# Streamed weights in DRAM: from slice by slice to partition by partition, 81 KB apart

## The chip, the cores and the metric

The kernel runs on one core of one Trainium2 chip. The metric is device time in microseconds (us) of one execution; the lower, the better. "PE" is TensorE, "DVE" VectorE, "ACT" ScalarE, "POOL" GpSimd and "SP" SyncE, whose queue issues the loads that this study is about.

## The reference, cut to what matters

Two branches read the same 2048 tokens of width 640 and are mixed by a gate. Branch A is attention with a sliding window. Branch B is recurrent: 64 segments of 32 tokens, each preceded by 8 memory tokens that the segment before has produced.

```python
for s in range(n_seg):                      # 64 segments, one after the other
    h = concatenate([mem, xs])              # 8 + 32 tokens
    q, k, v = h @ Wq, h @ Wk, h @ Wv        # each 640 x (32 heads * 192)
    ...                                     # softmax(q k^T) v
    o = o @ Wo                              # (32 * 192) x 640
    mem = o[:, :M]                          # needed by the next segment
```

The four matrices together take more room than the on-chip memory (SBUF) has left. Most slices of them stay resident; 21 slices are read from DRAM again in each segment.

## The kernel before

The streamed slices are packed once into a DRAM tensor `w_packed`. A slice is 128 partitions by 1536 bf16 values (q, k, v: 3072 B for a partition) or 1280 (o: 2560 B).

```python
KINDS = ("q", "k", "v", "o")
WQ, WO = 4 * 384, 2 * D

class Weights:
    def __init__(self, nc, dram, Wq, Wk, Wv, Wo, streamed):
        ...
        self.slot = {u: n for n, u in enumerate(streamed)}       # 21 slices
        self.packed = dram.tile([len(streamed), P, WQ], BF, name="w_packed")
    ...
    def dram_of(self, u):
        return self.packed[self.slot[u], :, 0:self.width(u)]
```

So a slice was one block of 384 KB, with the 128 rows one behind the other. The recurrent branch reads it into a ring of four buffers:

```python
sb = {"w": (4, [P, WQ]), ...}                                    # ring of 4
def load_w(u):
    if u not in weights.slot:
        return None                                              # resident
    b = sc.buf("w")
    sc.op("SP", 100 + 0.78 * weights.width(u),
          lambda: nc.sync.dma_start(tile_of(b)[:, 0:weights.width(u)], weights.dram_of(u)), writes=[b])
    return b
```

A fixed list schedule orders all instructions when the program is built; its costs are not measured on the chip, so the layout in DRAM does not alter the order.

## Time and profile before

| Quantity, kernel before | Value |
|---|---|
| time, median of 4 runs | 2614.36 us (2612.79 to 2619.13) |
| span of the profiled run | 2624.0 us |
| recurrent stage, from its first segment (the stream's first load is issued at 699.0 us) to 4 us after the issue of the last load | 708.6 to about 2588 us |
| one segment | 29.37 us |
| loads of the stream | 1344 (21 for each of 64 segments) |
| TensorE busy / DMA engines busy in the stage | 86% / 86% |
| chain of waits, loads of the stream | 32% of the span |

How to read it: the stage from 700 to 2590 us is most of the span, and in it both TensorE and the DMA engines are nearly full.

### The profile page before, as it was taken

What the parts mean: (1) busy time and instruction counts of PE and PEld (TensorE: products, weight loads), DVE (VectorE), ACT (ScalarE), POOL (GpSimd) and SP (SyncE); (2) the same over time, 40 slices, a digit from 0 to 9 for tenths busy, and PEclk for the clock granted to TensorE, in tenths of its full rate; (3) what the DMA queues carried; (4) which work ended last, traced back from release to release, by engine and by line L of the source; (5) the groups of instructions that cost most, each with busy time, mean ns of one, the idle gap of its engine ahead of it and who ended that gap; (6) DMA issues with size and microseconds to landing.
All of it is one profiled execution on the core that took longest, in us unless ns stands there. A gap on an engine that the chain in (4) does not pass through costs nothing.

```text
span 2624.0 us, 113795 instructions
## 1 busy us (share of the span) xinstructions
PE 2259.0 (86%) x49877; PEld 1665.6 (63%) x49893; DVE 1189.0 (45%) x3578; ACT 1115.8 (43%) x2433; POOL 602.1 (23%) x1782
## 2 busy tenths in 40 slices
PE   7888888899788888888888888888888888888885
PEld 5777777699465666666655665666666665566663
DVE  5777777623243344434443343434443444334433
ACT  5777777722233333333333333333333333334333
POOL 7622222040122222222222222222222222122220
PEclk9999999999899999989999998999999999999997
DMA  6600000085588888888888888888888888888887
GB/s 215 196 17 17 20 17 15 21 262 150 158 277 264 284 276 264 288 275 281 266 276 271 284 268 266 274 282 275 270 285 272 275 282 273 264 269 283 279 274 236
DMA packets 299154, 591.76 MB, mean 226 GB/s; under 512 B 102552, under 2 KB 112032, under 8 KB 298656
## 3 DMA queue, kind: packets, MB, share of 16 engines
q1 hardware_dynamic: 275536, 525.43, 63.6%
q0 software_dynamic: 20160, 55.60, 6.5%
q8 instruction: 391, 6.41, 1.0%
q10 hardware_dynamic: 2960, 3.44, 0.4%
q14 instruction: 107, 0.88, 0.1%
HBM read 554.98 MB, written 36.97 MB: 226 GB/s over the span
## 4 chain that ended last, share of the span: by engine, by line
PE 51%; DMA 35%; ACT 10%; DVE 2%; issue 2%; SPq 0%; ACTq 0%; POOL 0%; DVEq 0%
DMA t_w<-w_packed 32%; PE ps_q L597 8%; PE ps_k L597 8%; PE ps_o L762 7%; PE ps_v L597 5%; ACT a_ex L195 4%; PE t_psum L438 4%; ACT a_pt L208 3%; PE qk_ps L124 3%; PE ps_pv L738 2%; PE tr_k L612 2%; PE t_psv L455 2%; PE S_ps L666 2%; PE pt_ps L205 1%; PE s_ps L187 1%
## 5 line engine op out<-in xcount | busy, mean ns | idle before, releaser
L597 PEld LDWEIGHTS <-t_hT 128*32 128x32 bf16 x15360 | 380.0, 99 | 310.2 <-issue 105.8
L762 PE MATMUL ps_o<-t_OT,t_w 128*128 128x40 bf16 x6400 | 270.6, 182 | 124.9 <-DMA t_w<-w_packed 113.7
L762 PE MATMUL ps_o<-t_OT,w_o 128*128 128x40 bf16 x8960 | 334.6, 182 | 42.0 <-ACT t_OT L743 41.7
L762 PEld LDWEIGHTS <-w_o 128*128 128x128 bf16 x8960 | 289.1, 98 | 49.5 <-issue 43.5
L762 PEld LDWEIGHTS <-t_w 128*128 128x128 bf16 x6400 | 210.6, 98 | 155.4 <-DMA t_w<-w_packed 152.1
L743 ACT CAST t_OT<-ps_pv 128x480 bf16<-128x480 f32 x256 | 143.2, 559 | 340.2 <-PE ps_pv L738 339.9
L195 ACT ACTIVATE a_ex<-s_ps,a_nmx 128x384 bf16<-128x384 f32 (+2 forms) x512 | 252.8, 576 | 64.2 <-DVE a_nmx L193 61.5
L644 POOL COPY t_K<-t_xqk 128x64 bf16<-128x64 bf16 x256 | 60.8, 237 | 947.8 <-PE S_ps L666 665.6
L193 DVE TENSOR_REDUCE a_nmx<-s_ps 128x1 f32<-128x384 f32 (+2 forms) x512 | 246.7, 523 | 32.4 <-PE s_ps L190 24.8
L602 ACT CAST t_tok<-ps_k 128x384 bf16<-128x384 f32 x256 | 122.7, 479 | 319.5 <-PE ps_k L597 319.5
L597 PE MATMUL ps_q<-w_q,t_hT 128*32 128x384 bf16 x4096 | 230.4, 348 | 18.7 <-DVE t_hT L773 18.4
L721 DVE TENSOR_TENSOR t_PTx<-PT_ps,mk_x 128x320 bf16<-128x320 f32 x256 | 125.2, 489 | 264.7 <-PE PT_ps L714 264.7
L597 PE MATMUL ps_v<-w_v,t_hT 128*32 128x384 bf16 x4352 | 230.1, 335 | 0.0
L597 PE MATMUL ps_k<-w_k,t_hT 128*32 128x384 bf16 x4096 | 226.3, 343 | 0.3
L635 DVE COPY t_K<-tr_k 128x256 bf16<-128x256 bf16 x256 | 74.0, 289 | 253.7 <-PE tr_k L612 252.4
L602 ACT CAST t_tok<-ps_q 128x384 bf16<-128x384 f32 x256 | 123.0, 481 | 137.7 <-PE ps_q L597 137.5
L187 PE MATMUL s_ps<-KT_blk,QTm 128*128 128x128 bf16 x1440 | 171.0, 223 | 6.0 <-ACT a_ex L195 5.6
L602 ACT CAST t_vtok<-ps_v 128x384 bf16<-128x384 f32 x256 | 122.7, 479 | 114.2 <-PE ps_v L597 112.9
L612 PEld LDWEIGHTS <-t_tok 128*128 128x128 bf16 x1536 | 87.7, 98 | 118.7 <-ACT t_tok L602 55.4
L773 DVE CAST t_hT<-ps_o 128x40 bf16<-128x40 f32 x63 | 12.6, 200 | 327.1 <-PE ps_o L762 327.1
L205 PE MATMUL pt_ps<-a_ident,a_ex 128*128 128x128 bf16 x1440 | 145.6, 220 | 8.5 <-ACT a_ex L195 1.2
L676 DVE TENSOR_REDUCE sm_mx<-S_ps 128x4 f32<-128x160 f32 x256 | 82.5, 322 | 149.0 <-PE S_ps L666 149.0
(138 smaller groups left out, 4606.2 us busy)
## 6 DMA issues: line engine op xcount, KB each, us to landing
t_w<-w_packed SPq DMA_DIRECT2D x704, 384.0 KB, 4.4
t_w<-w_packed SPq DMA_DIRECT2D x640, 320.0 KB, 4.3
xbqk<-t_qk SPq DMA_DIRECT2D x16, 768.0 KB, 5.1
t_xqk<-xbqk POOLq DMA_DIRECT2D x64, 192.0 KB, 4.7
w_v<-in_B_Wv_dram POOLq DMA_DIRECT2D x17, 384.0 KB, 7.1
w_q<-in_B_Wq_dram POOLq DMA_DIRECT2D x16, 384.0 KB, 5.2
w_k<-in_B_Wk_dram POOLq DMA_DIRECT2D x16, 384.0 KB, 6.5
xbv<-t_vt SPq DMA_DIRECT2D x64, 96.0 KB, 1.8
```

The lines of the kernel that those rows point to most:

```text
L187: nc.tensor.matmul(sp[:, ci * P:(ci + 1) * P], lhsT=qm[r][:, g, :], rhs=kring[c][:, g, :], start=True, stop=not need_mask)
L193: nc.vector.tensor_reduce(out=nmx[:], in_=sp[:, 0:nk * P], axis=AX.X, op=ALU.max, negate=True)
L195: nc.scalar.activation(out=ex[:, 0:nk * P], in_=sp[:, 0:nk * P], func=ACT.Exp, bias=nmx[:], scale=1.0)
L205: nc.tensor.transpose(pt_ps[:, a, ci, :], ex[:, ci * P:(ci + 1) * P], ident[:])
L438: nc.tensor.matmul(pt[:, bb, :], lhsT=ws[ki][kt][:, c:c + P], rhs=xTb[:, kt, t * P:(t + 1) * P], start=(kt == 0), stop=(kt == KT - 1))
L597: nc.tensor.matmul(t[32 * j:32 * j + 32, 0:384], lhsT=tile_of(hT)[:, kt, :], rhs=w[:, j * 384:(j + 1) * 384], start=(kt == kts[0]), stop=( ...
L602: sc.op("ACT", act(384), lambda: nc.scalar.copy(tile_of(tok)[:], b["tile"][:, 0:384]), reads=[b], writes=[tok])
L612: nc.tensor.transpose(t[:, k, :], tok["tile"][:, k * P:(k + 1) * P], ident[:])
L676: nc.vector.tensor_reduce(out=x["mx"][:], in_=view(), axis=AX.X, op=ALU.max)
L721: nc.vector.tensor_tensor(out=tile_of(dst)[:], in0=PT["tile"][:, i, :, :].unsqueeze(2).to_broadcast([P, 2, 4, L]), in1=mk.unsqueeze(1).uns ...
L743: sc.op("ACT", act(480), lambda: nc.scalar.copy(tile_of(OT)[:].rearrange("p b j l -> p (b j l)"), o["tile"][:, 0:480]), reads=[o], writes= ...
L762: nc.tensor.matmul(t[:, dt * L:(dt + 1) * L], lhsT=w[:, r * D + dt * P:r * D + (dt + 1) * P], rhs=OT["tile"][:, b, i, :], start=(g == 0 an ...
```

## The change

The intent is to lay the streamed weights out by partition: in DRAM, all slices of partition 0 lie side by side, then those of partition 1, and so on. The tensor has 27 slots where 21 are used, so that neighbouring partitions are 27 x 3072 = 82944 B (81 KB) apart.

```diff
-        self.packed = dram.tile([len(streamed), P, WQ], BF, name="w_packed")
+
+        assert len(streamed) <= 27
+        self.packed = dram.tile([P, 27, WQ], BF, name="w_packed")
@@
     def dram_of(self, u):
-        return self.packed[self.slot[u], :, 0:self.width(u)]
+        return self.packed[:, self.slot[u], 0:self.width(u)]
```

## The prediction

> **What bounds the kernel now.** I read the page's slices first, then the stage table, the chain of waits, the DMA issues, and last the durations of single DMA packets.
>
> The slices show three phases: the sliding-window branch (to about 525 us, with next to no DMA from 128 us), the tail projections (525 to 700 us), and the recurrent branch (700 to 2590 us), which is 72% of the span.
>
> ```profile
> PE   7888888899788888888888888888888888888885
> ...
> DMA  6600000085588888888888888888888888888887
> GB/s 215 196 17 17 20 17 15 21 262 150 158 277 264 284 276 264 288 275 281 266 276 271 284 268 266 274 282 275 270 285 272 275 282 273 264 269 283 279 274 236
> ```
>
> Only the third phase streams weights all the time. The stage table (us, busy of PE, PEld, DVE, ACT, POOL, then clock, DMA share, GB/s) has for it:
>
> ```profile
> 700.00:2590.00 1890.00, 1634.09 (x40453) 1140.43 (x40453) 750.80 (x2627) 690.83 (x1603) 399.04 (x1369) 0.94 0.86 274
> ```
>
> Two things are nearly full at once: TensorE (1634 of 1890 us, 86%) and the 16 DMA engines (86%). Which of them ends the steps is told by the chain and by the waits:
>
> ```profile
> DMA t_w<-w_packed 32%; PE ps_q L597 8%; PE ps_k L597 8%; PE ps_o L762 7%; PE ps_v L597 5%; ACT a_ex L195 4%; PE t_psum L438 4%; ACT a_pt L208 3%; PE qk_ps L124 3%; PE ps_pv L738 2%; PE tr_k L612 2%; PE t_psv L455 2%; PE S_ps L666 2%; PE pt_ps L205 1%; PE s_ps L187 1%
> ...
> PEld L762 <- DMA t_w<-w_packed: 152.1, 269, 2.2
> ...
> PE ps_o L762 <- DMA t_w<-w_packed: 113.7, 178, 2.1
> ```
>
> The weight stream is the largest single item, 32% of the span or 840 us. TensorE idles for it too (113.7 us at the output projection, and some 39 us at the q, k and v matmuls). So the stage is bound by a loop of both: the stream goes through a ring of 4 buffers, and a load is issued when TensorE has finished with the buffer it overwrites. The queue that issues the loads shows it, waiting for TensorE and for landings in turn:
>
> ```profile
> SPq L565 <- PE ps_o L762: 327.6, 528, 2.4
> ...
> SPq L565 <- DMA t_w<-w_packed: 307.9, 446, 2.8
> ```
>
> The stream itself:
>
> ```profile
> t_w<-w_packed SPq DMA_DIRECT2D x704, 384.0 KB, 4.4
> t_w<-w_packed SPq DMA_DIRECT2D x640, 320.0 KB, 4.3
> ```
>
> That is 1344 loads, 21 for each of 64 segments. The copies of the new memory into t_hT start at 738.1 and at 2558.8 us, 62 segments apart, so a segment takes 29.37 us and a load comes every 1.40 us. With 4.35 us from issue to landing, 4.35/1.40 = 3.1 of the 4 buffers are in flight at any time.
>
> The records of single packets say how good these transfers are. The stage has 90107 packets of 3072 B and 81920 of 2560 B, one per partition row. Their medians, 121 and 102 ns, are practically their minimum: 3072/121 = 25.4 B/ns for one engine, 406 GB/s for 16. The means are 154.7 and 125.7 ns, because about one packet in ten stalls, mostly for 100 to 800 ns. In time of all 16 engines: (90107 x 154.7 + 81920 x 125.7)/16 = 1515 us of packets in the stage, of which 1204 us would be left with every packet at its median. **The stalls are 311 us, and only they can answer to where the rows lie in DRAM.** I sorted packets into 16 engines by fitting starts to ends (an inference, the record has no engine number). Packets that follow another without a gap hold 206 us of the stalls. Most of the rest follow a gap, where the delay of a first read is exposed; I don't expect the layout to change that.
>
> **What the Trainium skill says.** "Perfetto Trace Analysis", section "Contiguity and DMAs", says that contiguity matters only within an SBUF partition line. By that, 128 rows of 3072 B cost the same adjacent or 81 KB apart. The trace agrees only in part: rows are separate packets even now, though their DRAM bytes are adjacent, so no merging can be lost; nothing in it shows distant rows at this rate. "DMA: Bandwidth & Descriptors", section "Latency and other measured facts", reports that the row pitch does matter where it is a large power of two (207 GB/s at 512 KiB, 103 at 4 MiB, and full rate again with 4 KiB more). 81 KB = 82944 B is 81 x 1024, far smaller and an odd multiple, so that penalty should not be met. No trace here shows such a pitch. "HBM Reference", section "Specifications", gives about 716 GB/s for the memory that two cores share. This core alone draws 274 GB/s, so raw memory bandwidth is not short, which the 406 GB/s of the median packet supports.
>
> **The change part by part.**
> 1. Instructions. I compared the built programs engine by engine: the sequences are identical but for line numbers. The 1344 loads, their widths, the ring of 4, the queue and all waits stay. Removed: nothing; added: nothing. Issue stays about 320 ns a load on a queue that mostly waits. 0 us.
> 2. Packets. Each partition's row is still 3072 or 2560 B contiguous, so their number and the 1204 us at median stay. 0 us.
> 3. Filling the packed copy: 51 transfers of 80 or 384 KB at 77 to 123 us, DRAM to DRAM, with a scattered destination now. The stream's first read comes at 519 us, so even doubled times (2.7 to 9.1 us each) are hidden. 0 us.
> 4. First reads in the tail projections: 11 loads of 3.5 us. A change of 10% in each would be 4 us at most.
> 5. Stalls in the recurrent stage, the only real term. Before, one load reads a solid block of 384 KB, and the next in flight comes from another block. After, it reads 128 rows spread over 10.4 MB. In favour: streams of the 16 engines spread differently over memory, and the diff pads 21 slices to 27, so somebody chose the pitch with care; 21 slices would have given 63 KB, almost 64.[...] I choose a small gain, a quarter of the 206 us: 52 us of DMA time.
>
> How much of that reaches the end? The chain contains 840/4.35 = 193 landings, about 3 of the 21 in a segment. If a load needs x less DMA time, its landing, behind 3.1 in flight, comes about 3.1x earlier, and the chain gets 193 x 3.1x = 598x shorter, while DMA time falls by 1344x. **So about 0.45 of what the engines save reaches the end**; a slowdown could pass through fully, as DMA then becomes the sole bound. 52 x 0.45 = 23 us. With some weight for exactly nothing: 2614 - 16 = 2598 us.
>
> **Rivals.**
> - *Nothing happens.* The stalls come from refresh or from competing traffic, not from addresses. For it: they strike packets alike at all places, and the contiguous reads of t_xqk stall little less (146.8 ns mean against 154.7 for the same size). Time 2605 to 2620.
> - *Row conflicts vanish.* If half of the 206 us go, 103 x 0.45 = 46 us, 2568; if all 311 go, 140 us, 2474, the most this change can give by this sum. For it: 8% of packets stall even when they follow another without a gap. Against: no sign that one address is worse; the landing medians by position among the 21 loads lie within 4.1 to 4.7 us without order.
> - *Scattered rows are worse.* If the 206 us grow by half, 103 us more DMA time passes at 0.45 to 1: 2660 to 2717. For it: DMA share is 86%, with little slack. Against: large headroom in memory bandwidth.
> - *TensorE takes over.* With 86% busy in the stage, a faster stream can't remove more than the roughly 256 us that it idles, so this limits only the best case.
>
> **Range and chances.** Over 2% faster means 52 us at the end, so 116 us of DMA time, over half of the stalls without a gap. I give 0.27, more than the skill's page alone would allow, because of the deliberate 27. Over 2% slower means 52 to 116 us more stalls: 0.13. Within 2%: 0.60. Eight times in ten between 2535 and 2650 us.
>
> **What would show it.** In the profile after: the same 1344 loads with equal packet counts; median packets of 121 and 102 ns, and a mean of the 3072 B packets of about 149 instead of 154.7 ns; landing 4.2 us instead of 4.3 to 4.4; DMA share 0.84 to 0.87; the recurrent stage near 1870 us; the first 525 us unchanged. I'm wrong if the median packet moves (layout then acts on every read, not on stalls), if landing falls to about 3.5 us and TensorE's waits for the stream vanish, or if landing rises above 4.8 us.

## More of the kernel before

The prediction shows the lines. One part that it did not look at is the list of DMA queues (packets, MB, share of the time of 16 engines):

```profile
q1 hardware_dynamic: 275536, 525.43, 63.6%
...
q8 instruction: 391, 6.41, 1.0%
```

The stream is in the first line. The second is the fetching of instructions: 391 packets only, which will matter at the end (a second such queue, q14, is smaller: 107 packets, 0.88 MB).

## The result, and the profile after

The changed kernel took **2602.97 us** (median of 4 runs, 2600.24 to 2604.76), beside 2614.36 us before. The ratio is 0.9952, with a 95% interval of 0.9935 to 0.997. A ratio here is the mean time of one kernel's fast runs over that of the other's fast runs of the same rounds, so it is not quite the ratio of the medians. The result is correct.

The stage table (us, busy of PE, PEld, DVE, ACT, POOL, then clock, DMA share, GB/s) for the recurrent stage after:

```profile
700.00:2590.00 1890.00, 1631.96 (x40530) 1143.82 (x40527) 762.53 (x2641) 700.89 (x1618) 401.37 (x1373) 0.95 0.86 278
```

The DMA share is the same 0.86 and the rate rose from 274 to 278 GB/s. The stage now ends at about 2563 us, so this window already holds some of the final mixing. The chain of waits, the waits of TensorE for the stream and those of the issuing queue:

```profile
DMA t_w<-w_packed 30%; PE ps_o L764 8%; PE ps_q L599 8%; PE ps_k L599 8%; PE ps_v L599 5%; ACT a_ex L195 4%; PE t_psum L440 3%; ACT a_pt L208 3%; PE qk_ps L124 3%; PE ps_pv L740 2%; PE tr_k L614 2%; PE S_ps L668 2%; PE t_psv L457 1%; PE pt_ps L205 1%; PE S_ps L661 1%
```

```profile
PEld L764 <- DMA t_w<-w_packed: 136.7, 250, 2.0
PE ps_o L764 <- DMA t_w<-w_packed: 99.9, 159, 1.9
```

```profile
SPq L567 <- PE ps_o L764: 323.6, 540, 2.4
SPq L567 <- DMA t_w<-w_packed: 307.6, 443, 3.3
```

```profile
t_w<-w_packed SPq DMA_DIRECT2D x704, 384.0 KB, 4.3
t_w<-w_packed SPq DMA_DIRECT2D x640, 320.0 KB, 4.2
```

The columns of a wait are us in total, number of waits, longest one; those of a load its number, size and median us from issue to landing. Every line has the form that it had before: 30% of the chain instead of 32%, 99.9 us of waiting for the stream at the output projection instead of 113.7, median landings earlier by 0.1 us (mean landings by 0.03 us). Nothing new appears and nothing disappears. The question of the experiments is therefore whether the layout has done even this.

Two remarks on these two profiles. The profiled run of before took 2625.68 us, 11 us over that kernel's median, and the one of after 2601.72 us, 1 us under its own. So the pair exaggerates the difference. And time that differs by half a per cent must be set against how one kernel varies by itself: on the chip of the first four experiments the kernel before took 2605.87 to 2645.55 us in eleven runs (a granted TensorE clock, which is the share of its full clock that TensorE was given, of 0.948 in the shortest, 0.930 in the longest; the two go together in all three sets of eleven, which does not tell which is the cause). The longest of these counts as slow, being over 1.5% above the fastest, and is left out of the ratios; the longest fast run is 2641.37 us.

### The profile page after: what moved, and what is told of

Same layout as the page of the kernel before. It is cut to its first block, busy times and chain, and to the rows that moved or that the text cites. A ratio compares the mean times of both kernels' runs of the same rounds, so it can differ in the third digit from the quotient of the medians.

```text
span 2600.0 us, 113795 instructions
## 1 busy us (share of the span) xinstructions
PE 2249.0 (86%) x49877; PEld 1664.5 (64%) x49893; DVE 1190.4 (46%) x3578; ACT 1115.8 (43%) x2433; POOL 601.9 (23%) x1782
## 2 busy tenths in 40 slices
DMA packets 299154, 591.76 MB, mean 228 GB/s; under 512 B 102552, under 2 KB 112032, under 8 KB 298656
## 4 chain that ended last, share of the span: by engine, by line
PE 52%; DMA 34%; ACT 10%; DVE 2%; issue 2%; SPq 0%; POOL 0%; ACTq 0%; DVEq 0%; POOLq 0%
DMA t_w<-w_packed 30%; PE ps_o L764 8%; PE ps_q L599 8%; PE ps_k L599 8%; PE ps_v L599 5%; ACT a_ex L195 4%; PE t_psum L440 3%; ACT a_pt L208 3%; PE qk_ps L124 3%; PE ps_pv L740 2%; PE tr_k L614 2%; PE S_ps L668 2%; PE t_psv L457 1%; PE pt_ps L205 1%; PE S_ps L661 1%
## 5 line engine op out<-in xcount | busy, mean ns | idle before, releaser
L764 PE MATMUL ps_o<-t_OT,t_w 128*128 128x40 bf16 x6400 | 269.5, 182 | 111.5 <-DMA t_w<-w_packed 99.9
L193 DVE TENSOR_REDUCE a_nmx<-s_ps 128x1 f32<-128x384 f32 (+2 forms) x512 | 247.0, 524 | 33.7 <-PE s_ps L190 25.1
L604 ACT CAST t_tok<-ps_k 128x384 bf16<-128x384 f32 x256 | 122.7, 479 | 314.1 <-PE ps_k L599 314.1
L604 ACT CAST t_vtok<-ps_v 128x384 bf16<-128x384 f32 x256 | 122.7, 479 | 116.6 <-PE ps_v L599 115.2
```

The costliest lines, as they stand in the source:

```text
L193: nc.vector.tensor_reduce(out=nmx[:], in_=sp[:, 0:nk * P], axis=AX.X, op=ALU.max, negate=True)
L604: sc.op("ACT", act(384), lambda: nc.scalar.copy(tile_of(tok)[:], b["tile"][:, 0:384]), reads=[b], writes=[tok])
L764: nc.tensor.matmul(t[:, dt * L:(dt + 1) * L], lhsT=w[:, r * D + dt * P:r * D + (dt + 1) * P], rhs=OT["tile"][:, b, i, :], start=(g == 0 an ...
```

## The experiments

Theory A was the prediction's: DRAM reads stall, and the layout can act on nothing but these stalls; of what it saves about 0.45 reaches the end. The rival B: the stalls have nothing to do with the addresses, so the layout does nothing and half a per cent is chance. A third, C: the stalls arise where the data are written, not where they are read.

For all runs I took the durations of the stream's packets from the records, from the start of the first segment (708.6 us in the kernel before) to 4 us after the issue of the last load. "Packets" is their sum divided by 16 engines. "Stalls" is the part of it over the median of each size (121 ns for 3072 B and 102 ns for 2560 B; in e7 93 ns for its 2304 B, in e8 124 and 104 ns). "Landing" is the mean of the loads whose landing is recorded, about 1006 of 1344.

| Profile | mean ns, 3072 / 2560 B | packets, us | stalls, us | landing, us | segment, us | ratio of times (95%) |
|---|---|---|---|---|---|---|
| before | 154.7 / 125.7 | 1512 | 310 | 4.34 | 29.37 | - |
| e9, before again | 152.5 / 124.6 | 1494 | 293 | 4.32 | 29.11 | 0.9987 (0.9948 to 1.0026) |
| after | 151.5 / 122.7 | 1479 | 277 | 4.31 | 28.90 | 0.9952 (0.9935 to 0.997) |
| e1, after again | 154.4 / 123.5 | 1499 | 298 | 4.33 | 29.17 | 0.998 (0.993 to 1.0029) |
| e10, after a third time | 154.5 / 123.3 | 1498 | 297 | 4.30 | 29.24 | 0.9973 (0.993 to 1.0017) |
| e2, 63 KB | 154.4 / 124.0 | 1502 | 300 | 4.32 | 29.14 | 0.9938 (0.989 to 0.9986) |
| e3, 64 KB | 155.0 / 123.3 | 1501 | 300 | 4.30 | 28.93 | 0.994 (0.988 to 0.9999) |
| e4, rows apart | 153.7 / 123.7 | 1496 | 294 | 4.35 | 29.21 | 0.999 (0.9937 to 1.0042) |
| e6, same slot | 152.6 / 124.3 | 1493 | 292 | 4.31 | 29.11 | 0.994 (0.9901 to 0.9979) |
| e11, rows 4 KB | 151.4 / 123.4 | 1482 | 280 | 4.41 | 29.40 | 1.0039 (1.0004 to 1.0074) |
| e12, 512 KB | 151.9 / 121.9 | 1477 | 275 | 4.42 | 30.00 | 1.0121 (1.0075 to 1.0168) |
| e5, 2 MiB | 310.4 / 200.6 | 2769 | 1568 | 8.98 | 50.86 | 1.5382 (1.533 to 1.5434) |
| e7, thin loads | 122.6 (2304 B) / 128.1 | 1343 | 300 | 3.94 | 28.58 | 0.9807 (0.9776 to 0.9839) |
| e8, source in SBUF | 126.7 / 107.7 | 1262 | 34 | 3.89 | 27.91 | 0.9649 (0.9616 to 0.9681) |

Runs e1 to e4 shared one chip and its eleven runs of the kernel before (median 2633.49 us with the slow one), e5 to e8 a second (2619.61 us), e9 to e12 a third (2621.11 us).

### Is the gain there? e1, e9, e10

No edit: e1 and e10 are the changed kernel again, e9 is the kernel before against itself.

> The changed kernel once more, for a tighter interval beside the variants of this call. If the gain of half a per cent is real, the ratio is 0.993 to 0.998 again; if it came from one placement or from noise, it is 0.999 to 1.001. In the profile: packets of 3072 B with a mean of 151 to 152 ns against 154.7 ns before.

Measured: 2620.45 us, ratio 0.998; the 3072 B packets had a mean of 154.4 ns, not 151 to 152.

> The kernel before against itself, for a second profile on the chip of the next three and for the noise of a ratio. Ratio 0.997 to 1.003. If the stalls of the kernel before really are more than those of the changed one, its excess over the median packets is again about 310 us, against 277 and 298 us in two profiles of the changed kernel; if the difference was chance, it is 280 to 300 us.

Measured: 2622.99 us, ratio 0.9987; stalls 293 us, not 310.

> The changed kernel a third time, beside the kernel before against itself. If the layout saves 10 to 30 us of stalls, of which about a third reaches the end (170 us less DMA work gave 50 us, 250 us less gave 92 us), the time falls by 4 to 11 us, ratio 0.996 to 0.999. If nothing is saved, 0.998 to 1.002.

Measured: 2619.45 us, ratio 0.9973; stalls 297 us.

What follows: a ratio of the kernel before against itself can be 0.13% off one. The changed kernel gave 0.5, 0.2 and 0.3% less on three chips, in the same direction each time, but two of the three intervals include one. The stalls, 310 and 293 us before, are 277, 298 and 297 us after: their means, 302 and 291 us, differ by less than two profiles of one kernel do. The 154.7 ns that the prediction set out from was itself the high one of a pair. So a gain of 0.2 to 0.5% is possible and not established beyond the first chip.

### Does some part of the layout matter? e2, e3, e4, e6, e11

e2 drops the padding to 27 slots, so that partitions are 63 KB apart:

```diff
-        assert len(streamed) <= 27
-        self.packed = dram.tile([P, 27, WQ], BF, name="w_packed")
+        assert len(streamed) <= 21
+        self.packed = dram.tile([P, 21, WQ], BF, name="w_packed")
```

> The changed layout without the padding: 21 slots, so partitions 63 KB apart. If only the spreading of rows matters and no particular pitch, the ratio is that of the changed kernel, 0.993 to 0.998. If the pitch was chosen because 63 KB (almost 64) collides, it is 1.00 to 1.02, with a mean 3072 B packet above 155 ns.

Measured: 2612.8 us, ratio 0.9938, mean packet 154.4 ns. The padding shows no benefit for this stream.

e3 sets the pitch to exactly 64 KB (against the kernel before):

```diff
-        self.packed = dram.tile([len(streamed), P, WQ], BF, name="w_packed")
+        self.packed = dram.tile([P, 32768], BF, name="w_packed")
@@
-        return self.packed[self.slot[u], :, 0:self.width(u)]
+        n = self.slot[u] * WQ
+        return self.packed[:, n:n + self.width(u)]
```

> The same by-partition layout, partitions exactly 64 KB apart, a power of two. If row pitches of a power of two collide at this size already, the ratio is above 1.02 and the mean 3072 B packet above 165 ns. If the collision needs hundreds of KB, the ratio is 0.993 to 1.000, like the changed kernel.

Measured: 2607.04 us, ratio 0.994, mean packet 155.0 ns. A power of two of this size shows no harm.

e4 keeps rows 81 KB apart, but gives each slice its own region, so that slices of a partition are no longer adjacent:

```diff
-        self.packed = dram.tile([len(streamed), P, WQ], BF, name="w_packed")
+        self.packed = dram.tile([len(streamed), P, 27 * WQ], BF, name="w_packed")
```

> Rows of one slice 81 KB apart as in the changed kernel, but the slices of a partition not adjacent: each slice in its own 10.4 MB. If the gain comes from the distance of the rows, it stays: 0.993 to 0.998. If it comes from slices of a partition lying side by side, it goes: 0.999 to 1.003.

Measured: 2622.5 us, ratio 0.999, with an interval that holds both expectations. This one is inconclusive as to which half of the change did the little that was done.

e6 lets every load of the recurrent branch read the same solid block. Its result is wrong:

```diff
-        ... nc.sync.dma_start(tile_of(b)[:, 0:weights.width(u)], weights.dram_of(u)),
+        ... nc.sync.dma_start(tile_of(b)[:, 0:weights.width(u)], weights.packed[0, :, 0:weights.width(u)]),
```

> Wrong result on purpose: every load of the recurrent branch reads slice 0 of the old layout, one solid block of 384 KB, so no two loads in flight lie in different blocks. If stalls come from streams meeting in different rows of the memory, they shrink: excess over the median below 200 us instead of 310, ratio 0.96 to 0.985. If they do not come from addresses, excess 280 to 320 us and ratio 0.99 to 1.003. If 16 engines on the same small block collide, it is slower, above 1.01.

Measured: 2613.17 us, ratio 0.994, stalls 292 us. The stalls are those of the other layouts: streams that meet in different blocks are not what causes them. Its time is a little under my range's middle and even lower than that of e1, with the same stalls. I take that for the spread of runs, which no run separates further. But this interval excludes one, with the old rows and no spreading at all, so the same 0.994 in e2 and e3 is no proof of a gain by layout either.

The trace of e6 also settles a reading of the prediction, that landings have no order by position among the 21 loads of a segment. Only three of every four loads have a recorded landing, and the prediction's figures (4.1 to 4.7 us) come out when positions are counted among those alone. Counted over all loads (the sizes repeat every 21), the medians of the kernel before go from 3.55 us (tenth load) to 5.00 us (second load), in an order that returns in the changed kernel (3.57 to 5.05 us) and in e6 (3.62 to 5.02 us), where every load reads the same block. So the order belongs to the place in the segment and not to the address, and the conclusion that no address is worse stands.

e11 leaves the old order and only widens the rows from 3 to 4 KB:

```diff
-        self.packed = dram.tile([len(streamed), P, WQ], BF, name="w_packed")
+        self.packed = dram.tile([len(streamed), P, 2048], BF, name="w_packed")
```

> The old order, slice by slice, with rows at 4 KB instead of 3 KB, so rows are neither adjacent nor far apart. If any layout but an extreme one is the same to this stream, excess 280 to 310 us and ratio 0.994 to 1.003. If only far rows help, it equals the kernel before: excess about 310 us, ratio 0.999 to 1.003.

Measured: 2634.62 us, ratio 1.0039, stalls 280 us. The stalls are in my range, the ratio is just outside. It is slightly slower although its stalls are few: a load lands after 4.41 us in the mean instead of 4.32 us (e9). I had expected stalls and time to go together, and here they do not; e12 shows the same more strongly.

### Can the layout matter at all? e5, e12

These have the edit of e3 with another pitch: 1048576 elements (2 MiB) in e5, 262144 (512 KB) in e12.

> A layout that should hurt, as a control that layout can act here at all: partitions 2 MiB apart, slices of a partition adjacent. If the layout acts through collisions of rows at large powers of two, packets of 3072 B rise above 180 ns in the mean and the ratio is 1.05 to 1.3. If this stream does not feel the layout at all, the ratio is 0.99 to 1.01 and the mean stays 151 to 156 ns.

Measured: 4035.73 us, ratio 1.5382. The loads and TensorE's waits for the stream in its profile:

```profile
t_w<-w_packed SPq DMA_DIRECT2D x704, 384.0 KB, 9.1
t_w<-w_packed SPq DMA_DIRECT2D x640, 320.0 KB, 8.5
```

```profile
PEld L763 <- DMA t_w<-w_packed: 509.6, 379, 4.2
PE ps_o L763 <- DMA t_w<-w_packed: 462.8, 343, 4.1
PE ps_k L598 <- DMA t_w<-w_packed: 225.0, 171, 4.0
```

A load of the same bytes lands after 9.1 us instead of 4.4, and the output projection waits 462.8 us instead of 113.7. This is what a layout that hurts looks like: many more and longer stalls (1568 us; 29% of the packets are over 50 ns late instead of 10%), while the median packet is still 121 ns. With it the strict form of rival B falls, since stalls can answer to addresses; what remains of B is that they do not at the distances of the change. The median alone would have shown nothing. The harm was larger than my range.

> Slices of a partition adjacent, partitions 512 KB apart: between 64 KB, which cost nothing (ratio 0.994), and 2 MiB, which cost 1.54. If the harm starts only above 512 KB, as the skill's copies suggest (207 of 214 GB/s), ratio 0.99 to 1.02. If this stream of 3 KB rows feels it earlier, 1.05 to 1.3 with a mean 3072 B packet above 180 ns.

The copies meant are those of the passage on row pitch that the prediction cites.

Measured: 2654.14 us, ratio 1.0121. A harm of about one per cent shows at 512 KB and not at 64 or 81 KB. But the stalls, at 275 us, are the fewest of all runs that read DRAM (277 us in the first profile of the changed kernel). What grew is the time in which engines stand still between packets: the DMA share of its stage is 0.827 of 1918 us, so 332 us are idle, where e9 on the same chip has 0.862 of 1864 us, so 257 us. (The profiled run of e12 is the slowest of its four, at a granted clock of 0.923, so this exaggerates; but e11, profiled at 0.945 in the fastest of its runs, stands idle for 287 of 1882 us.) Loads also land later, 4.42 us after issue instead of 4.32, and idle engines cannot be why. Where this delay arises stays open: the first of a load's 16 semaphore increments comes 2.79 us after issue in e12 and 2.78 us in e9, and the packets are not longer. What the two runs show is that packet durations alone do not account for what a layout costs.

### Whose stalls are they, and what is a shorter load worth? e7, e8

e7 reads 3/4 of each row of q, k and v, and the matmuls use the third quarter twice (wrong result):

```diff
+    def part(u):
+        return weights.width(u) if u[0] == "o" else 3 * 384
@@
-        ... nc.sync.dma_start(tile_of(b)[:, 0:weights.width(u)], weights.dram_of(u)),
+        ... nc.sync.dma_start(tile_of(b)[:, 0:part(u)], weights.dram_of(u)[:, 0:part(u)]),
@@
-                                 rhs=w[:, j * 384:(j + 1) * 384],
+                                 rhs=w[:, (j if wb[kt] is None else min(j, 2)) * 384:][:, 0:384],
```

> Wrong result on purpose: the 704 loads for q, k and v read 3/4 of their row (2304 B instead of 3072 B), and the matmuls use the third quarter twice. That takes 704 x 128 x 30 ns / 16 = 170 us of DMA time from the stage of the kernel before. With the pass-through of 0.45 of the prediction the time falls by 77 us, ratio 0.970; if TensorE's clock and chain bound the stage instead, by under 30 us, ratio over 0.988; if the stream alone did, by 170 us, ratio 0.935.

Measured: 2574.08 us, ratio 0.9807, so 0.0193 x 2619.6 = 51 us less, between the first two of my three cases and in neither. Its loads, TensorE's waits for them, and the start of its chain of waits:

```profile
t_w<-w_packed SPq DMA_DIRECT2D x640, 320.0 KB, 4.0
t_w<-w_packed SPq DMA_DIRECT2D x704, 288.0 KB, 3.7
```

```profile
PEld L765 <- DMA t_w<-w_packed: 153.8, 240, 2.2
PE ps_o L765 <- DMA t_w<-w_packed: 121.0, 171, 2.1
```

```profile
DMA t_w<-w_packed 25%; PE ps_q L600 9%; PE ps_o L765 9%; PE ps_k L600 9%; PE ps_v L600 6%; ACT a_ex L195 4%; PE t_psum L438 4%; ACT a_pt L208 3%; PE qk_ps L124 3%; PE ps_pv L741 3%; PE tr_k L615 2%; PE t_psv L455 2%; PE S_ps L669 2%; PE out_ps L255 1%; PE S_ps L662 1%
```

The packets' time fell to 1343 us, by 151 to 169 us against the two profiles of before. So 0.30 to 0.34 of it reached the end. The wait at the output projection did not fall at all (121.0 us, 113.7 in the kernel before). The stalls stayed at 300 us in total although a quarter of the bytes of the q, k and v packets was gone. Per packet, these lost 29.6 ns to stalls instead of 31.5 to 33.7, so most of a stall did not go with the bytes.

e8 takes the DRAM away: the loads copy a resident weight tile inside SBUF, in the same shapes and numbers (wrong result):

```diff
-        ... nc.sync.dma_start(tile_of(b)[:, 0:weights.width(u)], weights.dram_of(u)),
+        ... nc.sync.dma_start(tile_of(b)[:, 0:weights.width(u)], weights.tiles["q", 0, 0][:, 0:weights.width(u)]),
```

> Wrong result on purpose: the loads of the recurrent branch copy a resident weight tile inside SBUF, same shape and number, so they read no DRAM. If the stalls belong to reading DRAM, they go: excess under 60 us, mean packet within 5 ns of the median, time down by 0.45 x 250 to 310 us = 110 to 140 us, ratio 0.945 to 0.96. If they come from the writing side (SBUF busy with the engines' accesses, or the queues), the excess stays near 300 us and the ratio is 0.99 to 1.01.

Measured: 2531.99 us, ratio 0.9649, so 0.0351 x 2619.6 = 92 us less, the fastest of all, though less than the 110 to 140 us that I expected. The loads and the waits for them:

```profile
t_w<-w_q SPq DMA_DIRECT2D x704, 384.0 KB, 3.9
t_w<-w_q SPq DMA_DIRECT2D x640, 320.0 KB, 3.9
```

```profile
PEld L762 <- DMA t_w<-w_q: 114.2, 230, 2.0
PE ps_o L762 <- DMA t_w<-w_q: 79.6, 133, 1.9
```

The stalls are gone but for 34 us, and packets over 50 ns late are 2% instead of 10%. That all loads read one tile is not why, since e6 does so too, in DRAM, with 292 us of stalls. So the stalls belong to reading DRAM, as theory A has it, and C falls. But TensorE still waits 79.6 us for the stream at the output projection, and a load still needs 3.9 us. The packets' time fell by 232 to 250 us, and 92 us of that, 0.37 to 0.40, reached the end. This is about the most that a perfect DRAM layout could have given. It is no strict bound, because the median packets from SBUF are 3 and 2 ns longer: a DRAM stream without any stall would need 1512 - 310 = 1202 us of packets instead of 1262, and with the same share passed on that would be some 115 us (an estimate).

The program's four buffers and its schedule hold in every variant, and no correct version that clearly beats both kernels came out of these runs; e2 and e3 are level with the changed kernel within their intervals.

### What holds up the last engine

The loads of e8 have hardly any stalls and still take 3.9 us. The records of a load's semaphore have 16 increments, which I take as one for each of the 16 DMA engines, and they suggest why. One load of e8, issued 747.2 us into the span, after the data of the loads before it and more than 2.9 us before the data of the next:

```
increments of its semaphore, us after issue (16 engines)
2.40 2.43 2.44 2.46 2.47 2.48 2.50 2.51 2.52 2.54 2.55 2.56 2.58 2.59 2.60    3.92
packet of the instruction queue (16384 B): starts 0.95, takes 1.06, ends 2.01
120 data packets (15 engines x 8) start from 1.12 to 2.13; the other 8 from 2.00 on
```

Fifteen engines are done within 0.2 us of each other. The last is 1.3 us late. Its data packets start just when the packet of 16 KB of instructions ends, 0.9 us after those of the others, and its first three take 246, 334 and 258 ns instead of about 124. That the same engine carried both is inferred from these times, as the records name no engine. The queue line of the profile quoted above had 391 of these packets; 317 fall into the recurrent stage, with a mean of 1.09 us in the kernel before, never two at once. In that kernel, the 257 loads without such a packet between 0.8 us after issue and their landing landed after 3.99 us in the mean, the 749 with one after 4.46 us. The fifteenth engine differs by only 0.12 us between the two (3.76 and 3.88 us). This grouping exaggerates, since a load that lands late has more time to meet such a packet. With a fixed stretch of 0.8 to 3.0 us after issue, it is 4.19 us (432 loads) against 4.45 us (574), and the fifteenth engine shows no delay (3.87 and 3.84 us). This is a correlation in one profile and one example in another, not an experiment: no run took the instructions away. The changed kernel has the same packets (317, 1.05 us) and the same gap (3.94 and 4.44 us). The second instruction queue, with 78 packets of 0.42 us in the stage, is not counted here. Whether it is always the same engine of the 16 the records do not tell; if it is, that engine would be busy for about 1512 + 345 = 1857 of the 1879 us of the stage (an estimate from the two sums), and would be what this stage is bound by. No run tested that.

## Why the prediction was right or wrong

The time was predicted at 2598 us and came out at 2602.97, within 2% with the chance of 0.60. By its steps:

- **Steps 1 and 2, same instructions and packets: right.** The page shows the same packet counts, 299154 in total, and medians of 121 and 102 ns.
- **Steps 3 and 4, packing and tail projections: right.** The stretch from 128 to 525 us has 346.86 us of PE work after and 347.29 before. The stream's first read comes at 522.8 us instead of 519.0, and the first load of the stage is issued at 702.8 us instead of 699.0, within what e1 to e12 show (698.8 to 706.7 us in all but e5).
- **Step 5, a quarter of 206 us of stalls saved: mis-sized.** I put 52 us there. The first pair of profiles gives 310 - 277 = 33 us, all five profiles of the two kernels give 11 us. The measured mean of the 3072 B packets was 151.5, 154.4 and 154.5 ns, where I had said 149.
- **"Only they can answer to where the rows lie": wrong as a step.** e12 has fewer stalls than any other kernel that reads DRAM and is 1.2% slower; its loads land later and its engines stand still for longer, and packet durations show neither. The accounting by packet durations is incomplete, though it identified the right side: e8 shows that the stalls come from reading DRAM.
- **A pass-through of 0.45: too high.** It measured 0.30 to 0.34 in e7 and 0.37 to 0.40 in e8. The first half of the argument held: in e7 a load needs x = 151 to 169 us / 1344 = 0.11 to 0.13 us less and lands 0.38 to 0.40 us earlier, 3.2 to 3.4 times x, where I had said 3.1. What failed is that the 193 landings on the chain stay there. In e7 the stream is 25% of a span of 2583.3 us, which at 3.94 us is 164 landings: as it got faster, other work took its place. That is only part of the shortfall: 164 landings of 3.2 to 3.4 times x would still be 0.39 to 0.41 of the DMA time, and the rest stays unexplained. With 11 us and 0.30 to 0.40, the layout would be worth 3 to 4 us, with 33 us 10 to 13 us. The measured 0.2 to 0.5% are 5 to 13 us.
- **Other readings of the prediction.** That landings are without order by position is a miscount, shown under e6. The 206 us of stalls in packets without a gap and their 8% come out again when I redo the sort; packets of 3072 B after a gap take 204 ns in the mean, those without 146. The 10.4 MB are 10368 KB, so 10.6 million bytes.
- **The number itself: partly luck.** 2598 us is 5 us off while both factors of its gain were too large; the weight given to "exactly nothing" took back 7 of the 23 us, and one kernel's runs spread over more than 5 us.
- **The deliberate 27 as a sign of a gain: no support.** 63 KB (e2) does as well. The weight that I gave it went into the chance of 0.27.
- **Rivals.** "Nothing happens" is closest to the truth: the changed kernel ends 2 us below the 2605 to 2620 that I wrote for it. "Scattered rows are worse" holds only for pitches far above this one. "TensorE takes over" did not occur, even in e8.
- **What would show it.** Landing 4.2 to 4.3 us, DMA share 0.86, first 525 us unchanged: as written. The recurrent stage, counted as the prediction did from the first load to the last output projection, took 1861 us in the profile (702.8 to 2563.5) where I had written about 1870, partly because the two profiled runs lie on opposite sides of their medians.

What stays open is whether the half per cent on the first chip is the layout's. Three ratios under one speak for it, the stalls of the repeated profiles do not, and e6 reaches 0.994 without it.

## What to carry to other kernels

In a stream like this one, with packets at their minimum in the median and DRAM rows of 3 KB, moving the rows from 3 to 81 KB apart was worth nothing that one can rely on; keep clear of the pitches that cost something here (512 KB 1.2%, 2 MiB 54%), and judge by means and landings, since the median packet hides the harm. Before estimating what a faster stream is worth, measure the pass-through with a run that loads less: here only 0.30 to 0.40 of the saved DMA time reached the end. And look at the last of the 16 engines, not at their mean, when asking why a load lands late.

## What the Trainium skill lacked or had wrong

- "Perfetto Trace Analysis", section "Contiguity and DMAs": that contiguity matters only within an SBUF partition line held for rows 3 to 81 KB apart (ratios 0.994 to 1.004), but not at a pitch of 512 KB (1.0121) or 2 MiB (1.5382). The section lacks the exception.
- "DMA: Bandwidth & Descriptors", section "Latency and other measured facts", on row pitch: its rates are for DRAM-to-DRAM copies of 16 KiB rows, with 207 GB/s at 512 KiB and 164 at 2 MiB, a quarter more time. For loads of 3 KB rows into SBUF the runs show more harm at 2 MiB: the packets' time rose from 1512 to 2769 us, a factor of 1.83, with the median packet unchanged at 121 ns.
- The same page has no number for how often single packets stall and for how long: with nothing unusual in the layout, 10% of the packets took over 50 ns more than the median, by 279 ns in the mean, when read from DRAM, and 2% did when read from SBUF (e8).
- "Runtime: NRT & Kernel Launch", section "Instruction fetch mechanics", says that instructions come in blocks of 16 KiB by a DMA queue of their own and that the cost is mostly hidden. The trace agrees on the blocks for the larger of two instruction queues: 391 packets of 16384 B; the smaller has blocks of 8192 B. It lacks what they cost other transfers: a packet takes about 1.09 us, and loads that meet one from 0.8 to 3.0 us after issue land after 4.45 us instead of 4.19 (a correlation).
